# Scores of a chunked linear attention in four 64x64 tiles of TensorE, without the block above the diagonal

## The chip, the core and the metric

The kernel runs on one core of a Trainium2 chip. The metric is the device time of one execution in microseconds; of the runs of the kernel before, three are shown. An execution that the hardware profiler took is shown beside them: its time is compared with its own span, and all durations below come from it.

The engines are named as in the profile: PE (TensorE, matrix products), PEld (its weight loads), DVE (VectorE), ACT (ScalarE), POOL (GpSimd), SP (SyncE, which issues all loads and stores). Every engine works off its own list of instructions in order, and waits on semaphores for the others.

## The reference

A recurrence over 768 tokens for 4 batches and 8 heads of 48 channels, and behind it a two-layer network over all 3072 tokens (384 to 2048 to 384 channels):

```python
    for t in range(S):
        kt, vt, rt = (k[:, :, t], v[:, :, t], r[:, :, t])
        cur = np.einsum('bhd,bhe->bhde', u[None] * kt, vt)
        y[:, :, t] = np.einsum('bhd,bhde->bhe', rt, state + cur)
        state = w[None, :, :, None] * state + np.einsum('bhd,bhe->bhde', kt, vt)
...
    h = x @ w_in
    g = np.maximum(h, 0.0) + alpha * np.minimum(h, 0.0)
    return (g @ w_out).astype(np.float32)
```

## The kernel before, in words

**Attention.** The 768 tokens are cut into 6 chunks (`c`) of 128, and the heads into 4 pairs (`q`), which gives 24 stages; one call of `attention(c, q, at)` writes one stage. A stage loads `r` and `k0` (channels on the partitions: head 0 of the pair on partitions 0 to 47, head 1 on 64 to 111) and `v` and `k` (tokens on the partitions). DVE multiplies `r` and `k0` by tables of decay (L348). PE forms the scores `A[g]`, for each head `g` of the pair and each of the 4 batches a product of 128 by 128 tokens over 48 channels in f32 (L388, 8 products). Only scores of an earlier token with a later one are wanted, and the diagonal has a value of its own, `cu`. So ACT writes `base`, the identity scaled by `cu` (L395, 8 instructions), and DVE copies the scores above the diagonal into it under the mask `strict` (L399, `copy_predicated`, one instruction of 512 columns for each head). PE then multiplies state and `r` (L435), `v` and `base` (L440), and adds to the state (L449); in chunks 0 and 1 the first two are L429 and L424. ACT and DVE split the result into a high and a low part `xh`, `xl` (L482, L483).

In chunks 0 and 1 `cu` comes from a product on PE (L363: it needs `uw`, which POOL makes of the loaded `up` and `wp`, L242, and the product `prod` of DVE, L356); from chunk 2 on from POOL (L373, L375) and DVE (L379).

**Network.** 96 steps, each with 9 products of 512 columns into `hp` (L530) and 9 into `acc` (L561). ACT and DVE make the activations between them (L536, L537, L540, L541). The weights are split into high and low parts while the first steps run, one of 16 pieces at a time (L291 to L302; `wraw` is their load).

**Order.** Nothing runs in the order of the code. Each piece of work is given to a planner (`Plan`) with an engine, an assumed duration and a rank; it lists them by a simulation of its own and writes them out in that order. A piece whose assumed duration changes, a buffer pool of another size or an added piece can therefore move others on every queue. At the start, before there are products to do, PE is given small products of the identity (L621) to fill its waits. The pool `raw` (6 buffers) holds `r` and `k0`; those of stage 3 of chunk 0 lie in the pool `o`.

## Time and profile before

| | us |
|---|---|
| three runs, median (lowest to highest) | 525.99 (523.62 to 526.05) |
| the profiled execution, its time | 525.11 |
| the profiled execution, its span from first to last instruction | 523.4 |
| PE busy in it | 511.0 |
| DVE busy | 318.7 |
| ACT busy | 242.4 |
| POOL busy | 43.4 |

The time of an execution is its span and 1.7 us around it. A busy engine is read against a stretch, not the whole: an engine that is busy over half the span can be full in one stretch and idle in another. PE's rows overlap, since a product's end is modelled and the next begins before it; what one group of products costs is read from its first start to the first start of the next group.

### The profile page before, as it was taken

To read this page: it belongs to the slowest core of one execution; us is meant where nothing else is said; L and a number is where in the kernel's file an instruction comes from. 1 tells how busy PE (TensorE), PEld (TensorE's weight loads), DVE (VectorE), ACT (ScalarE), POOL (GpSimd) and SP (SyncE) were. 2 spreads that over 40 slices of the span, in tenths; PEclk is the share of its full clock that TensorE was granted. 3 is DMA by queue.
4 is the path that set the end of the run, shared out by engine and by line. 5 is a ranking of instruction groups with operands and counts; after the bars stand their busy time and mean duration, and the time that the engine had idled before them with its cause. 6 is when DMAs were issued, how large, how long until landed. Compare 5 with 4: busy or idle time off the path is not lost.

```text
span 523.4 us, 8460 instructions
## 1 busy us (share of the span) xinstructions
PE 511.0 (98%) x3288; PEld 406.3 (78%) x3288; DVE 318.7 (61%) x513; ACT 242.4 (46%) x525; POOL 43.4 (8%) x45
## 2 busy tenths in 40 slices
PE   7999999999999999999999999999999999999995
PEld 5877787888878777887787877877777778888883
DVE  5698999999556685854764654573544443333331
ACT  2766666658445352542552643552534332432222
POOL 1000030001012021120110102030000000000000
PEclk9699999999999999999999999999999999999998
DMA  8766666362232541422220323120120000100001
GB/s 224 271 180 195 209 195 206 107 224 91 74 107 81 168 144 35 145 69 66 75 61 20 111 71 88 48 82 1 35 92 2 0 1 2 60 0 1 0 1 64
DMA packets 24877, 47.22 MB, mean 90 GB/s; under 512 B 4096, under 2 KB 12416, under 8 KB 24832
## 3 DMA queue, kind: packets, MB, share of 16 engines
q1 hardware_dynamic: 24832, 46.62, 28.2%
q8 instruction: 28, 0.46, 0.4%
q14 instruction: 17, 0.14, 0.1%
HBM read 37.96 MB, written 6.29 MB: 85 GB/s over the span
## 4 chain that ended last, share of the span: by engine, by line
PE 93%; DMA 2%; DVE 2%; SPq 1%; issue 1%; ACT 0%; POOL 0%; ACTq 0%; POOLq 0%
PE acc L561 38%; PE hp L530 38%; PE A L388 5%; PE y L440 2%; PE y L435 2%; PE A L440 1%; PE acc L621 1%; PE y L424 1%; DMA wraw<-wall 1%; PE y L449 1%; DMA up<-uP 1%; PE acc L363 1%; PE y L429 1%; PE acc L388 1%; PE y L363 1%; DVE wx L298 1%
## 5 line engine op out<-in xcount | busy, mean ns | idle before, releaser
L537 DVE SCALAR_TENSOR_TENSOR g<-hp,alph,g 128x512 f32<-128x512 f32 x96 | 71.9, 749 | 127.0 <-ACT g L536 127.0
L536 ACT ACTIVATE g<-hp 128x512 f32<-128x512 f32 x96 | 57.3, 597 | 155.0 <-PE hp L530 154.7
L530 PE MATMUL hp<-xh,wh 128*128 128x512 f32 x288 | 116.3, 404 | 0.0
L530 PE MATMUL hp<-xl,wh 128*128 128x512 f32 x288 | 113.9, 395 | 0.3 <-DVE xl L483 0.3
L530 PE MATMUL hp<-xh,wl 128*128 128x512 f32 x288 | 114.0, 396 | 0.0
L540 ACT ACTIVATE gh<-g 128x512 fp32r<-128x512 f32 x96 | 60.5, 631 | 68.2 <-DVE g L537 68.1
L541 DVE TENSOR_TENSOR gl<-g,gh 128x512 fp32r<-128x512 f32 x96 | 66.6, 693 | 39.4 <-ACT gh L540 39.4
L561 PE MATMUL acc<-gh,wh 128*128 128x512 f32 x288 | 85.2, 403 | 0.6 <-ACT gh L540 0.6
L561 PE MATMUL acc<-gl,wh 128*128 128x512 f32 x288 | 83.2, 396 | 0.0
L561 PE MATMUL acc<-gh,wl 128*128 128x512 f32 x288 | 83.1, 395 | 0.0
L530 PEld LDWEIGHTS hp<-xh,wh 128*128 128x128 f32 x288 | 54.1, 188 | 13.9 <-issue 0.4
L530 PEld LDWEIGHTS hp<-xl,wh 128*128 128x128 f32 x288 | 54.2, 188 | 13.6 <-DVE xl L483 0.8
L561 PEld LDWEIGHTS acc<-gl,wh 128*128 128x128 f32 x288 | 54.1, 188 | 13.1
L561 PEld LDWEIGHTS acc<-gh,wl 128*128 128x128 f32 x288 | 54.1, 188 | 12.9
L561 PEld LDWEIGHTS acc<-gh,wh 128*128 128x128 f32 x288 | 52.5, 188 | 14.4 <-ACT gh L540 1.3
L530 PEld LDWEIGHTS hp<-xh,wl 128*128 128x128 f32 x288 | 54.2, 188 | 12.1
L395 ACT ACTIVATE base<-ident,cu 128x128 f32<-128x128 f32 x192 | 60.0, 390 | 0.2
L373 POOL TENSOR_TENSOR rr<-rr,kk 128x384 f32<-128x384 f32 x16 | 22.5, 1408 | 298.6 <-DMA kk<-vkr 180.1
L348 DVE TENSOR_TENSOR raw<-raw,W 112x512 f32<-112x512 f32 x46 | 35.5, 787 | 0.8 <-DMA raw<-rk 0.8
L399 DVE COPY_PREDICATED base<-strict,A 128x512 f32<-128x512 uint8 x44 | 30.3, 730 | 3.6 <-ACT base L395 1.8
L388 PEld LDWEIGHTS A<-raw 48*128 48x128 f32 x352 | 22.1, 193 | 8.3 <-issue 6.2
L388 PE MATMUL A<-raw 48*128 48x128 f32 x352 | 26.3, 290 | 1.3 <-DVE raw L348 1.3
(90 smaller groups left out, 420.8 us busy)
## 6 DMA issues: line engine op xcount, KB each, us to landing
wraw<-wall SPq DMA_DIRECT2D x16, 768.0 KB, 5.2
raw<-rk SPq DMA_DIRECT2D x46, 224.0 KB, 3.2
v<-vkr SPq DMA_DIRECT2D x24, 192.0 KB, 3.2
kk<-vkr SPq DMA_DIRECT2D x24, 192.0 KB, 2.7
rr<-vkr SPq DMA_DIRECT2D x16, 192.0 KB, 2.4
oT<-o SPq DMA_DIRECT2D x12, 256.0 KB, 2.2
oT<-g SPq DMA_DIRECT2D x6, 256.0 KB, 2.3
xh<-xh SPq DMA_DIRECT2D x36, 32.0 KB, 2.0
```

The source lines that it names most:

```text
L348: add("DVE", 0.72, lambda t=t, tab=tab: nc.vector.tensor_tensor(out=t(), in0=t(), in1=tab().broadcast_to([112, B, L]), op=ALU.mult), r=[W[ ...
L373: add("POOL", 1.2, lambda: nc.gpsimd.tensor_tensor(out=rt(), in0=rt(), in1=k(), op=ALU.mult), r=[k] + ([wh[12]] if c == 2 else []), w=[rt] ...
L388: nc.tensor.matmul(A[g]()[:, b], k0()[half(g), b], r()[half(g), b], start=(b == 0), stop=(b == B - 1), skip_group_check=True)
L395: add("ACT", 0.39, lambda g=g, b=b: nc.scalar.activation(base[g]()[:, b], ident(), AF.Copy, scale=cu()[:, g, b:b + 1]), r=[cu, ident], w=[ ...
L399: add("DVE", 0.75, lambda g=g: nc.vector.copy_predicated(base[g](), strict()[:, None, :].broadcast_to([128, B, L]), A[g]()), r=[strict, A[ ...
L440: nc.tensor.matmul(y[g]()[half(o), j * L:(j + 1) * L], v()[:, g * B + b], base[g]()[:, b], start=False, stop=(j == 1), skip_group_check=True)
L530: nc.tensor.matmul(hp(), a[i]()[:, k], x[c]()[:, k], start=(k == 0 and j == 0), stop=(k == NK - 1 and j == 2))
L536: add("ACT", 0.6, lambda: nc.scalar.activation(g(), hp(), AF.Copy), r=[hp], w=[g], rank=n - 100)
L537: add("DVE", 0.75, lambda: nc.vector.scalar_tensor_tensor(out=g(), in0=hp(), scalar=alph()[:, i:i + 1], in1=g(), op0=ALU.mult, op1=ALU.max ...
L540: add("ACT", 0.64, lambda: nc.scalar.activation(gh(), g(), AF.Copy), r=[g], w=[gh], rank=n - 100)
L541: add("DVE", 0.73, lambda: nc.vector.tensor_tensor(out=gl(), in0=g(), in1=gh(), op=ALU.subtract), r=[g, gh], w=[gl], rank=n - 99)
L561: nc.tensor.matmul(banks[k](), a[i]()[:, NK + k], x(), start=(begin and j == 0), stop=(end and j == 2))
```

## The change

Chunks 0 and 1 keep their products, masks and layout but for the order of the batches in `v`, `k` and `r`. From chunk 2 on (16 stages):

- The scores are formed by `triangle()`. Each product of 128 by 128 tokens becomes two: earlier tokens 0 to 63 with all 128 later ones, and earlier tokens 64 to 127 with later ones 64 to 127. The fourth block, earlier tokens 64 to 127 with later ones 0 to 63, is left out. Each product uses 48 channels and 64 columns of weights, so that it takes one of four quarters of PE; four stand in a row that use four different quarters (two heads, two batches).
- So that two batches can write the two halves of the partitions of one bank at a time, batches 1 and 3 have the two halves of a chunk's tokens swapped on the partitions. The host lays `v`, `k` and `r` of these batches out that way (`np.roll` by 64) and orders the batches 0, 2, 1, 3; `place` finds them. ACT writes `base` with its halves swapped, POOL makes a mask `strict4` with the swap in it and a second, swapped copy of the table `wtok` (`swapped_masks`), and `scale_k` reads the table with both.
- DVE's two copies under the mask become six: for each head the later tokens 64 to 127 on all partitions (256 columns), and for the even and for the odd batches the later tokens 0 to 63 on half the partitions (128 columns).
- The pool `raw` has 5 buffers; `k0` of stage 2 of chunk 0 lies in the pool `gl`.
- The planner is told 0.85 us for the scores in place of 1.1, and 0.42, 0.28 and 0.28 us for the copies of a head in place of 0.75.

```diff
+    strict4 = fixed([128, B, L], "strict4", U8)
...
-    wtok, w128, unit = fixed([128, H, D], "wtok"), fixed([112, P], "w128"), fixed([112, 65], "unit")
+    wtok, w128, unit = fixed([128, H, 2, D], "wtok"), fixed([112, P], "w128"), fixed([112, 65], "unit")
...
+    def swapped_masks():
+        add("POOL", 0.3, lambda: nc.gpsimd.memset(ones(), 1.0), w=[ones], rank=10)
+        for rows, base in ((slice(0, HI), -HI), (slice(HI, 128), 0)):
+            add("POOL", 0.3, lambda rows=rows, base=base: nc.gpsimd.affine_select(
+                ones()[rows], ones()[rows], pattern=[[1, 128]], base=base, channel_multiplier=-1,
+                compare_op=ALU.is_gt, fill=0.0), w=[ones], rank=10)
+        for b in range(B):
+            add("POOL", 0.3, lambda b=b: nc.gpsimd.tensor_copy(strict4()[:, b], (ones if b % 2 else strict)()),
+                r=[ones, strict], w=[(strict4, b)], rank=10)
+        for h in range(2):
+            add("POOL", 0.5, lambda h=h: nc.gpsimd.tensor_copy(
+                wtok()[HI * h:HI * h + HI, :, 1], wtok()[HI - HI * h:128 - HI * h, :, 0]), r=[(wtok, 0)],
+                w=[(wtok, 1 + h)], rank=10)
...
-        r, k0 = (sb([112, B, L], *(("o", 2) if first and q == P - 1 else ("raw", 6)))
-                 for _ in range(2))
+        place = [0, 2, 1, 3]
+        def swap(b):
+            return c > 1 and b % 2 == 1
+        r, k0 = (sb([112, B, L], *(("o", 2) if first and q == P - 1 else ("gl", 3) if first and q == 2 and j else
+                                   ("raw", 5))) for j in range(2))
...
+        def triangle():
+            for rows, j in ((0, 0), (0, 1), (1, 0), (1, 1)):
+                for b, g in ((2 * j, 0), (2 * j + 1, 0), (2 * j, 1), (2 * j + 1, 1)):
+                    o, t = (rows + b) % 2, slice(HI * rows, L)
+                    nc.tensor.matmul(A[g]()[HI * o:HI * o + HI, b, t], k0()[half(g), b, HI * rows:HI * rows + HI],
+                                     r()[half(g), b, t], start=(rows == 0 and j == 0), stop=(rows == 1 and j == 1),
+                                     skip_group_check=True)
         def scores():
+            if c > 1:
+                return triangle()
...
-        add("PE", 1.1, scores, r=[r, k0], w=A, rank=10 * q - 90 if first else at)
+        add("PE", 1.1 if c < 2 else 0.85, scores, r=[r, k0], w=A, rank=10 * q - 90 if first else at)
...
-                    base[g]()[:, b], ident(), AF.Copy, scale=cu()[:, g, b:b + 1]), r=[cu, ident], w=[(base[g], b)],
+                    base[g]()[:, b].rearrange("p (a t) -> p a t", a=2),
+                    ident().rearrange("p (a t) -> p a t", a=2)[:, ::-1 if swap(b) else 1], AF.Copy,
+                    scale=cu()[:, g, (b if c < 2 else place[b]):][:, 0:1]), r=[cu, ident], w=[(base[g], b)],
...
+        parts = [(slice(0, 128), slice(0, B), slice(HI, L)), (slice(0, HI), slice(0, B, 2), slice(0, HI)),
+                 (slice(HI, 128), slice(1, B, 2), slice(0, HI))]
+        for g, at_part in [(g, x) for g in range(2) for x in parts] if c > 1 else ():
+            add("DVE", 0.42 if at_part is parts[0] else 0.28, lambda g=g, x=at_part: nc.vector.copy_predicated(
+                base[g]()[x], strict4()[x], A[g]()[x]), r=[strict4, A[g]], w=[base[g]], rank=at - 1.5)
+        for g in range(2) if c < 2 else ():
...
-                    nc.tensor.matmul(y[g]()[half(o), j * L:(j + 1) * L], v()[:, g * B + b], base[g]()[:, b],
+                    nc.tensor.matmul(y[g]()[half(o), j * L:(j + 1) * L], v()[:, g * B + place[b]], base[g]()[:, b],
...
-            k4 = k().rearrange("p (g b) e -> p g b e", g=2)
+            table = wtok()[:, 2 * q:2 * q + 2, 0] if c < 2 else \
+                wtok()[:, 2 * q:2 * q + 2].rearrange("p h s e -> p (h s) e")
+            k4 = k().rearrange("p (n b) e -> p n b e", n=2 if c < 2 else 4)
...
+    swapped_masks()
...
-    vkr = np.ascontiguousarray(vkr.transpose(4, 2, 5, 0, 3, 1, 6)).reshape(C, H // 2, L, 3 * 2 * B * D)
+    vkr = vkr.transpose(4, 2, 5, 0, 3, 1, 6)[:, :, :, :, :, [0, 2, 1, 3]]
+    vkr = np.ascontiguousarray(vkr)
+    vkr[2:, :, :, :, :, 2:] = np.roll(vkr[2:, :, :, :, :, 2:], HI, axis=2)
+    vkr = vkr.reshape(C, H // 2, L, 3 * 2 * B * D)
```

What the planner makes of it is shown at three places. First PE's list, at the scores of chunk 2, pair 1; `hp` and `acc` belong to the network, `A0` and `A1` are the scores of the two heads. Before, the two rows of L388 stand four times in turn:

```order
L530 MATMUL hp_1712<-xl_426,wh14_98 128x512
L388 MATMUL A0_1727<-raw_961,raw_976 128x128
L388 MATMUL A1_1729<-raw_961,raw_976 128x128
L561 MATMUL acc0_1582<-gh_1627,wh12_96 128x512
L561 MATMUL acc1_1584<-gh_1627,wh12_96 128x512
```

And now, where each of the four rows of L411 stands twice, the two of 64x128 ahead of the two of 64x64, and `x2` is two batches:

```order
L571 MATMUL hp_1731<-xl_432,wh14_99 128x512
L411 MATMUL A0_1746<-raw_970,raw_1093 64x128 x2
L411 MATMUL A1_1749<-raw_970,raw_1093 64x128 x2
L411 MATMUL A0_1746<-raw_970,raw_1093 64x64 x2
L411 MATMUL A1_1749<-raw_970,raw_1093 64x64 x2
L602 MATMUL acc0_1601<-gh_1646,wh12_97 128x512
```

8 products have become 16 in the same place between the same products of the network. Second DVE's list, at a stage of chunk 3 (`T0` is the state, `xl0` the low part of the result; L537 and L541 belong to the network). Before:

```order
L537 SCALAR_TENSOR_TENSOR g_2193<-hp_2172,alph_71,g_2193 128x512
L541 TENSOR_TENSOR gl_2214<-g_2193,gh_2202 128x512
L399 COPY_PREDICATED base_1977<-strict_69,A0_2204 128x512
L399 COPY_PREDICATED base_2006<-strict_69,A1_2206 128x512
L537 SCALAR_TENSOR_TENSOR g_2231<-hp_2216,alph_71,g_2231 128x512
L541 TENSOR_TENSOR gl_2268<-g_2231,gh_2240 128x512
```

And now, where each row of 64x2x64 stands twice, for the even and the odd batches:

```order
L578 SCALAR_TENSOR_TENSOR g_2248<-hp_2229,alph_72,g_2248 128x512
L582 TENSOR_TENSOR gl_2277<-g_2248,gh_2257 128x512
L435 COPY_PREDICATED base_2020<-strict4_70,A0_2259 128x4x64
L435 COPY_PREDICATED base_2049<-strict4_70,A1_2262 128x4x64
L435 COPY_PREDICATED base_2020<-strict4_70,A0_2259 64x2x64
L435 COPY_PREDICATED base_2049<-strict4_70,A1_2262 64x2x64
L578 SCALAR_TENSOR_TENSOR g_2298<-hp_2279,alph_72,g_2298 128x512
```

Two copies have become six in the same place, and the network's next instruction stands behind them as before. Third SP's list of loads at the program's start, behind the first three loads of `raw`. Before:

```order
L221 DMA wp_64<-wP 112x4
L328 DMA raw_171<-rk 112x512
L328 DMA raw_173<-rk 112x512
L328 DMA o_175<-rk 112x512
L222 DMA up_65<-uP 112x4
L328 DMA raw_178<-rk 112x512
```

And now:

```order
L223 DMA wp_64<-wP 112x4
L349 DMA raw_170<-rk 112x512
L224 DMA up_65<-uP 112x4
L349 DMA o_177<-rk 112x512
L349 DMA raw_180<-rk 112x512
L349 DMA gl_186<-rk 112x512
```

The small load of `up` has moved two places ahead: one load of 112x512 stands between it and `wp`, where three stood. POOL's seven instructions for `strict4` stand ahead of `uw` on its list, and the two for `wtok` behind it. Between 20 and 100 us the planner has also exchanged neighbours on PE, DVE and SP in chunk 1; the visits of PE to products of another tile shape than the network's have become one more there.

## Rows read from the trace of the kernel before

**Rows 1.** The page: busy time of the engines; the chain that ended last, by engine.

```profile
PE 511.0 (98%) x3288; PEld 406.3 (78%) x3288; DVE 318.7 (61%) x513; ACT 242.4 (46%) x525; POOL 43.4 (8%) x45
...
PE 93%; DMA 2%; DVE 2%; SPq 1%; issue 1%; ACT 0%; POOL 0%; ACTq 0%; POOLq 0%
```

**Rows 2.** Stretches: length, busy us (instructions) of each engine, granted clock, DMA share, GB/s.

```profile
12.00:22.00 10.00, 9.73 (x67) 8.45 (x67) 5.89 (x15) 6.40 (x23) 0.00 (x0) 0.50 0.97 319
22.00:34.00 12.00, 11.73 (x138) 9.77 (x136) 11.29 (x18) 9.54 (x26) 0.00 (x0) 1.00 0.46 141
34.00:57.50 23.50, 21.76 (x202) 16.36 (x198) 22.11 (x35) 14.28 (x31) 0.00 (x0) 1.00 0.64 192
57.50:91.00 33.50, 33.50 (x288) 26.77 (x288) 33.25 (x49) 21.89 (x46) 5.94 (x4) 1.00 0.64 211
91.00:130.00 39.00, 39.00 (x175) 31.45 (x172) 37.74 (x60) 27.08 (x51) 2.24 (x2) 1.00 0.45 147
200.00:300.00 100.00, 100.00 (x675) 79.24 (x674) 59.72 (x100) 44.26 (x102) 11.80 (x10) 1.00 0.24 74
```

**Rows 3.** PE in order of time (start, us) around one stage's scores.

```profile
257.57 0.39 PE L530 MATMUL hp<-xh,wl 128*128 128x512 f32 x1
257.80 0.40 PE L530 MATMUL hp<-xl,wh 128*128 128x512 f32 x1
258.13 1.16 PE L388 MATMUL A<-raw 48*128 48x128 f32 x16
259.22 0.97 PE L561 MATMUL acc<-gh,wh 128*128 128x512 f32 x3
```

**Rows 4.** The scores' products by line: duration ns min/median/max, first and last start.

```profile
L388 PE MATMUL A<-raw x352: 271/272/579, 8.5 to 420.2; 48*128 48x128 f32 x176
```

**Rows 5.** PE in order of time at the same stage's products behind the scores.

```profile
263.61 0.31 PE L435 MATMUL y<-raw,T 48*48 48x128 f32 x1
263.63 0.31 PE L435 MATMUL A<-raw,T 48*48 48x128 f32 x1
263.76 0.27 PE L435 MATMUL y<-raw,T 48*48 48x128 f32 x1
263.87 0.27 PE L435 MATMUL y<-raw,T 48*48 48x128 f32 x1
263.98 0.27 PE L435 MATMUL y<-raw,T 48*48 48x128 f32 x1
264.20 0.31 PE L440 MATMUL y<-base,v 128*48 128x128 f32 x1
...
265.11 0.61 PE L449 MATMUL y<-v,kk 128*64 128x48 f32 x16
265.65 0.96 PE L561 MATMUL acc<-gh,wh 128*128 128x512 f32 x3
```

**Rows 6.** Groups by line: count, busy us, mean ns of one, idle before.

```profile
L399 DVE COPY_PREDICATED base<-strict,A 128x512 f32<-128x512 uint8 x44 | 30.3, 730 | 3.6 <-ACT base L395 1.8 <-PE A L388 1.8
L483 DVE TENSOR_TENSOR xl<-A,xh 48x256 fp32r<-48x256 f32 x32 | 13.5, 423 | 4.5 <-ACT xh L482 3.3
L375 POOL TENSOR_TENSOR rr<-rr,utab 128x384 f32<-128x384 f32 x16 | 18.7, 1169 | 1.3
```

**Rows 7.** DVE in order of time behind the scores of rows 3.

```profile
259.60 1.35 DVE L399 COPY_PREDICATED base<-strict,A 128x512 f32<-128x512 uint8 x2
260.84 0.67 DVE L541 TENSOR_TENSOR gl<-g,gh 128x512 fp32r<-128x512 f32 x1
264.41 0.75 DVE L537 SCALAR_TENSOR_TENSOR g<-hp,alph,g 128x512 f32<-128x512 f32 x1 [2.90 <-ACT g L536]
```

**Rows 8.** The chain that ended last, at the start: start, us, what.

```profile
4.09 5.51 DMA up<-uP
...
10.59 1.05 PE acc L363 x8
```

**Rows 9.** DVE and POOL at the start, in order of time, with waits.

```profile
5.74 0.48 DVE L247 TENSOR_TENSOR_SCAN W<-wp,unit 112x65 f32<-112x65 f32 x2 [4.59 <-DMA wp<-wP]
...
8.92 0.69 DVE L356 TENSOR_TENSOR g<-raw 112x512 f32<-112x512 f32 x1
...
1.82 0.29 POOL L237 CAST strict<-ones 128x128 uint8<-128x128 f32 x1
...
9.75 0.79 POOL L242 TENSOR_TENSOR uw<-up,wp 48x4 f32<-48x4 f32 x2 [7.56 <-DMA up<-uP]
```

More of the change, by code (lines that the diff above doesn't have):

```diff
@@ L265, in token_table @@
         add("DVE", 0.4, lambda: nc.vector.tensor_copy(
-            wtok().rearrange("p (m g) e -> p m g e", g=2), pt()[:, :, :, 0:D]), r=[pt], w=[wtok], rank=-30)
+            wtok()[:, :, 0].rearrange("p (m g) e -> p m g e", g=2), pt()[:, :, :, 0:D]), r=[pt], w=[(wtok, 0)], rank=-30)
     raws = {}
@@ L395, in attention @@
                 add("ACT", 0.39, lambda g=g, b=b: nc.scalar.activation(
-                    base[g]()[:, b], ident(), AF.Copy, scale=cu()[:, g, b:b + 1]), r=[cu, ident], w=[(base[g], b)],
+                    base[g]()[:, b].rearrange("p (a t) -> p a t", a=2),
+                    ident().rearrange("p (a t) -> p a t", a=2)[:, ::-1 if swap(b) else 1], AF.Copy,
+                    scale=cu()[:, g, (b if c < 2 else place[b]):][:, 0:1]), r=[cu, ident], w=[(base[g], b)],
                     rank=at - 0.9 if c != 1 else -50)
-        for g in range(2):
+        parts = [(slice(0, 128), slice(0, B), slice(HI, L)), (slice(0, HI), slice(0, B, 2), slice(0, HI)),
[4 more added lines that the diff above has]
+        for g in range(2) if c < 2 else ():
             add("DVE", 0.75, lambda g=g: nc.vector.copy_predicated(
@@ L422, in out @@
                     for g in range(2):
-                        rows, x = (slice(0, HI) if g == 0 else half(g)), g * B + b
+                        rows, x = (slice(0, HI) if g == 0 else half(g)), g * B + place[b]
                         nc.tensor.matmul(y()[rows, b], v().rearrange("p x e -> p (x e)")[
@@ L447, in state_product @@
                 for g in range(2):
-                    rows, x = slice(HI * g, HI if g == 0 else HI + D), g * B + b
+                    rows, x = slice(HI * g, HI if g == 0 else HI + D), g * B + place[b]
                     nc.tensor.matmul(u_rows(rows)[:, b], kt[:, x * D:x * D + rows.stop - rows.start], vt[:, x],
@@ L456, in scale_k @@
         def scale_k():
-            k4 = k().rearrange("p (g b) e -> p g b e", g=2)
+            table = wtok()[:, 2 * q:2 * q + 2, 0] if c < 2 else \
+                wtok()[:, 2 * q:2 * q + 2].rearrange("p h s e -> p (h s) e")
+            k4 = k().rearrange("p (n b) e -> p n b e", n=2 if c < 2 else 4)
             nc.vector.tensor_tensor(out=k4, in0=k4, op=ALU.mult,
-                                    in1=wtok()[:, 2 * q:2 * q + 2, None, :].broadcast_to([128, 2, B, D]))
+                                    in1=table[:, :, None, :].broadcast_to(list(k4.shape)))
         if first:
@@ L464, in attention @@
             if not last:
-                add("DVE", 0.56, scale_k, r=[wtok], w=[k], rank=at - 1.6)
+                add("DVE", 0.56, scale_k, r=[(wtok, 0)] if c < 2 else [wtok], w=[k], rank=at - 1.6)
             add("PE", 1.7 if last else 2.3, out if last else both, r=[T[q], r, v] + base + ([] if last else [k]),
@@ L510, in state @@
                 U = pb([112, B * D], "y")
-                add("DVE", 0.56, scale_k, r=[wtok], w=[k], rank=0.5 * q - 1)
+                add("DVE", 0.56, scale_k, r=[(wtok, 0)], w=[k], rank=0.5 * q - 1)
                 add("PE", 0.8, state_product, r=[k, v], w=[U], rank=0.5 * q - 1)
```

## The prediction

> **What bounds the kernel now.** I read the page's busy times first, then the stretches, then PE's own timeline. The page gives PE 511.0 us of a span of 523.4, and the chain of work that ended last runs through PE for 93% of the span; no other engine is over 61% [rows 1]. A mean over stages says little, so the second view is the stretches [rows 2]: from 57.5 us on PE's busy time equals the length of every stretch shown (33.50 of 33.50, 39.00 of 39.00, 100.00 of 100.00), at a granted clock of 1.00, which is 2.4 GHz. There PE waits for nobody, and a microsecond less of work on PE is a microsecond less of time. Before 57.5 it is otherwise: between 34 and 57.5 PE is busy for 21.76 of 23.50 us and DVE for 22.11, between 22 and 34 DVE for 11.29 of 12, and from 57.5 to 91 DVE is as full as PE (33.25 of 33.50). All 16 stages that the change touches lie behind chunk 1, in the part that PE bounds; the change reaches the first 57 us only through the planner.
>
> **The scores on PE.** One stage before: its 16 records (8 products, two records each) begin at 258.13 and the network's next product at 259.22, so the scores hold PE for 1.09 us [rows 3]. The scores' rows on `A` number 352 [rows 4], with 32 more on other banks for the 24 stages, so 16 a stage everywhere.
>
> One stage after has 32 records. The nearest row for the first 16 (64 columns of weights, 128 columns passed through, 48 rows, four quarters of PE) is L435, which works in the same four quarters on the same `raw` with 48 columns of weights: it begins at 263.61, the next line at 264.20, so 0.59 us for 16 records, with entry and exit [rows 5]. The four quarters start within 0.02 us of each other (263.61 to 263.63), and the steps of one quarter follow at 0.11 us (263.76, 263.87, 263.98). The 16 columns more of weights count once, ahead of the first step; a third of what the first step is longer by (263.76 - 263.61 - 0.11 = 0.04) makes 0.01.
>
> The other 16 records pass 64 columns instead of 128, in four further steps. Upper bound of a step: 0.11, as if the shorter pass gained nothing. Lower bound: half, 0.055. Which one holds depends on whether 64 columns of weights can be loaded into each quarter at that pace. L449 shows it for two halves of PE: 16 records, 8 in each half, one half with 64 columns of weights and 48 passed; the first starts at 265.11, the last at 265.11 + 0.61 - 0.22 = 265.50 (0.22 for the length of one record), which is 7 steps of 0.056 [rows 5]. I take 0.056, since it is the row with the same weights.
>
> So a stage after is 0.59 + 0.01 + 4 x 0.056 = 0.82, between 0.82 and 0.59 + 0.01 + 4 x 0.11 = 1.04. Gain: 1.09 - 0.82 = 0.27 at best, 0.05 at worst. Entry and exit are the same before and after: a product of the network stands on either side, as before. I round down to 0.26, as four quarters with short passes are shown by no row: **16 x 0.26 = 4.2 us**, with 0.8 as the other end.
>
> A rule of the Trainium skill speaks against this: "TensorE: Matmul & The Clock Gate", section "Wait — 56ns, not 53.3ns?", says that products never start less than about 25 ns apart however short they are. By it the 16 short records would take 0.40 us, the stage 1.00, and the gain would be an estimated 16 x 0.09 = 1.4 us. The trace disagrees for quarters that are free: four starts within 0.02 us [rows 5].
>
> **DVE.** Two copies of 512 columns at 0.73 us become six [rows 6]. No row shows the smaller ones. A copy of 256 columns out of a PSUM bank takes 0.42 in L483 [rows 6]; by the slope between the two (0.31 for 256 columns) one of 128 columns takes 0.27, and at most 0.42. A stage then costs 2 x (0.42 + 2 x 0.27) = 1.92 to 2 x 3 x 0.42 = 2.52 in place of 1.46: 0.5 to 1.1 us more, 7 to 17 us in all. None of it is on the path. Behind the copies DVE sits idle for 2.90 us ahead of 264.41, and the copies end at 260.95 where L440, which reads them, begins at 264.20 [rows 5, 7]: 3.25 us of cover for 1.1. Queued behind the copies is L541 (260.84), whose result is used steps later. Without the cover the price would be the whole 17 us. In the fullest stretch (91 to 130, DVE 37.74 of 39.00 [rows 2]) lies one stage's set, whose 0.5 to 1.1 still fits in 1.26.
>
> **ACT** writes the same 8 blocks with halves swapped. Even at twice the price it would stay off the path: ACT is busy for 44 of 100 us [rows 2]. `scale_k` multiplies the same number of elements. Counted at nothing.
>
> **POOL and the loads at the start.** Seven instructions for `strict4` stand ahead of `uw` on POOL: by L237's 0.29 us [rows 9] 2.0 us at most. POOL waits there for 7.56 us for `up` [rows 9], which hides them; without that wait they would delay `uw` by 2.0. And `up` itself is now two loads earlier. `wp` landed at about 5.7 us, when DVE's L247 could start [rows 9], `up` at 9.60 [rows 8], with three loads of 224 KB between: 1.3 us each. With one between, `up` lands near 7.0 and `uw` is ready near 7.9. The first L363 then waits for `prod` (L356, 8.92 + 0.69 = 9.61 [rows 9]) and starts near 9.7 instead of 10.59 [rows 8]. This is the head of the chain that ended last, so I take **0.9 us** off; between nothing (if a later wait, for ACT or a load, takes its place) and more (see the clock, below).
>
> **What the planner moved between 20 and 100 us.** One more visit of PE to another tile shape costs about 0.2 us: 0.33 between 257.80 and 258.13 where the network's step is 0.23, and the same again behind it [rows 3]. POOL's two copies for `wtok` run right behind DVE's making of that table in chunk 0, at most 1.17 each (L375 [rows 6]), while DVE is nearly full; nobody waits for them until chunk 2, but the two can slow each other. And neighbours on DVE's list have been exchanged where it is full. I bound this sum by -0.5 and +1.5 and take **+0.5**.
>
> Sum, against the profiled execution: 525.1 - 4.2 - 0.9 + 0.5 = 520.5. The median of the runs is 0.9 above that execution, 525.99. Halfway between them is 525.5, from which the sum gives 520.9; I forecast **521.0**, and count the rivals from 525.5 too.
>
> **The rivals.**
> - *Short products gain nothing much.* The 0.024 us from record to record in L449 (0.39 us for 16) is also what one would see if PE could not start records faster in a sustained row. Then the 16 short records take 0.39 in place of 0.22, or, at the upper bound above, 0.44: a stage of 0.99 to 1.04, a gain of 0.8 to 1.6 us. For it: no row has 32 such records. Against it: in L449 the weights of 64 columns explain the same step. Time: 525.5 - 1.2 - 0.4 = 523.9. This is also how the change would fail to do what it says.
> - *The clock does not fall at the start.* From 12 to 22 us PE runs at 0.50, 1.2 GHz, and DVE is busy for only 5.89 of 10 us [rows 2]; ahead of it PE waited for `raw` and for `uw`. With `uw` early, PE's wait shrinks by 0.9, and the clock may stay up. PE's 10 us of work would take 5; DVE's 4.1 idle us cap the gain. Half of the cap, 2, on top of the forecast: 519.0.
> - *A wait opens in 34 to 57.5.* There DVE has 1.4 us to spare in 23.5 [rows 2], and its order has changed. If PE waits there for a split piece of weights for as long as it did ahead of 12 us (some 2 us in all), the clock can fall again for as long as it did then: ten microseconds at half, 5 us. With the start's gain lost as well, 525.5 - 4.2 + 0.5 + 5 = 526.8, slower than before. Against it: DVE's work ahead of the weights is the same but for about one instruction.
>
> **How the numbers follow.** The forecast has 0.58 (519.5 to 522.8), the short products 0.19, the clock 0.14, the wait 0.09. The range should leave out the wait and the tails: 518.3 to 524.3. About 0.5% (2.6 us) is what a measurement of this kernel can tell from no change. Forecast and clock lie below 523.4 with little exception, 0.70; the short products are within, with the forecast's tail and half of the third rival's, 0.24; slower is the rest, 0.06.
>
> **What would show it.** In the profile after: a stage's scores from first start to the network's next product at 0.80 to 0.85 (0.99 or more: the first rival); the quarters' short steps at 0.056; PE's busy time equal to the stretches from about 57 us on; L363's first start near 9.7; L435's copies done before L440. The prediction is wrong if PE shows waits behind 57.5 us, if the last product of chunk 1 ends later than before, or if the short steps are 0.1 us.

## The result: 517.3 us, below the range

The changed kernel takes 517.30 us (median of its runs, 516.91 to 518.28); the runs of the kernel before beside it have a median of 524.81 (520.12 to 526.05). The ratio is 0.9874, with a 95% interval of 0.9844 to 0.9905: 1.3% shorter, clear of noise, by more than the forecast of 521.0, and below the range of 518.3 to 524.3. Over the 70 runs of the kernel before that stand beside the experiments its median is 523.77, so the 525.5 from which the forecast counted was 1.7 too high: the first fault of the prediction, and one that no view of a single profile shows.

### The profile page after: what moved, and what is told of

The parts are those of the page before. It is cut to its first block, busy times and chain, and to the rows that moved or that the text cites. A ratio compares the mean times of both kernels' runs of the same rounds, so it can differ in the third digit from the quotient of the medians.

```text
span 515.2 us, 9052 instructions
## 1 busy us (share of the span) xinstructions
PE 504.3 (98%) x3544; PEld 400.8 (78%) x3544; DVE 328.2 (64%) x577; ACT 242.8 (47%) x525; POOL 46.9 (9%) x54
## 4 chain that ended last, share of the span: by engine, by line
PE 93%; DVE 3%; ACT 1%; DMA 1%; issue 1%; SPq 0%; DVEq 0%; ACTq 0%
PE acc L602 39%; PE hp L571 39%; PE A L411 3%; PE y L479 2%; PE y L474 2%; PE A L479 1%; PE A L420 1%; PE y L463 1%; PE y L488 1%; PE y L468 1%; ACT base L427 1%; DMA wp<-wP 1%; PE acc L384 1%; DVE raw L369 1%; PE acc L662 1%
## 5 line engine op out<-in xcount | busy, mean ns | idle before, releaser
L571 PE MATMUL hp<-xh,wh 128*128 128x512 f32 x288 | 115.7, 402 | 0.8 <-DMA xh<-xh 0.8
L571 PE MATMUL hp<-xl,wh 128*128 128x512 f32 x288 | 113.8, 395 | 0.0
L571 PE MATMUL hp<-xh,wl 128*128 128x512 f32 x288 | 113.7, 395 | 0.0
L582 DVE TENSOR_TENSOR gl<-g,gh 128x512 fp32r<-128x512 f32 x96 | 68.6, 714 | 41.5 <-ACT gh L581 41.3
L602 PE MATMUL acc<-gh,wh 128*128 128x512 f32 x288 | 85.2, 402 | 0.2 <-ACT gh L581 0.2
L602 PE MATMUL acc<-gh,wl 128*128 128x512 f32 x288 | 83.3, 396 | 0.0
L602 PE MATMUL acc<-gl,wh 128*128 128x512 f32 x288 | 82.7, 394 | 0.0
L571 PEld LDWEIGHTS hp<-xh,wh 128*128 128x128 f32 x288 | 54.0, 188 | 14.4 <-DMA xl<-xl 0.9
L602 PEld LDWEIGHTS acc<-gl,wh 128*128 128x128 f32 x288 | 54.0, 188 | 12.8
L602 PEld LDWEIGHTS acc<-gh,wl 128*128 128x128 f32 x288 | 53.8, 188 | 13.0
L571 PEld LDWEIGHTS hp<-xl,wh 128*128 128x128 f32 x288 | 54.1, 188 | 12.7
L571 PEld LDWEIGHTS hp<-xh,wl 128*128 128x128 f32 x288 | 54.1, 188 | 12.0
L602 PEld LDWEIGHTS acc<-gh,wh 128*128 128x128 f32 x288 | 52.4, 188 | 13.3 <-ACT gh L581 0.7
L394 POOL TENSOR_TENSOR rr<-rr,kk 128x384 f32<-128x384 f32 x16 | 20.4, 1273 | 275.0 <-DMA kk<-vkr 136.5
L369 DVE TENSOR_TENSOR raw<-raw,W 112x512 f32<-112x512 f32 x45 | 36.7, 832 | 0.0
L435 DVE COPY_PREDICATED base<-strict,A 64x128 f32<-64x128 uint8 (+1 forms) x96 | 26.9, 343 | 0.8
L524 DVE TENSOR_TENSOR xl<-y,xh 48x256 fp32r<-48x256 f32 (+1 forms) x38 | 17.5, 462 | 3.0 <-ACT xh L523 2.6
L396 POOL TENSOR_TENSOR rr<-rr,utab 128x384 f32<-128x384 f32 x16 | 19.2, 1202 | 1.3
```

The source lines that it names most:

```text
L369: add("DVE", 0.72, lambda t=t, tab=tab: nc.vector.tensor_tensor(out=t(), in0=t(), in1=tab().broadcast_to([112, B, L]), op=ALU.mult), r=[W[ ...
L394: add("POOL", 1.2, lambda: nc.gpsimd.tensor_tensor(out=rt(), in0=rt(), in1=k(), op=ALU.mult), r=[k] + ([wh[12]] if c == 2 else []), w=[rt] ...
L396: add("POOL", 1.2, lambda: nc.gpsimd.tensor_tensor(out=rt().rearrange("p (g b) e -> p g b e", g=2), in0=rt().rearrange("p (g b) e -> p g b ...
L435: add("DVE", 0.42 if at_part is parts[0] else 0.28, lambda g=g, x=at_part: nc.vector.copy_predicated(base[g]()[x], strict4()[x], A[g]()[x] ...
L524: add("DVE", us + 0.1, lambda: nc.vector.tensor_tensor(out=view(l), in0=psum(), in1=view(h), op=ALU.subtract), r=[src] + refs(h), w=refs(l ...
L571: nc.tensor.matmul(hp(), a[i]()[:, k], x[c]()[:, k], start=(k == 0 and j == 0), stop=(k == NK - 1 and j == 2))
```

## The profile after

The profiled execution took 516.91 us, 515.2 of them in the span. In the changed file the scores of chunk 2 and on are L411 (those of chunks 0 and 1 stay in L420), the network's products L571 and L602, the products with `uw` L384, the new predicated copies L435, the products behind the scores L474, L479 and L488. The page's busy times and its chain by engine (answering rows 1):

```profile
PE 504.3 (98%) x3544; PEld 400.8 (78%) x3544; DVE 328.2 (64%) x577; ACT 242.8 (47%) x525; POOL 46.9 (9%) x54
PE 93%; DVE 3%; ACT 1%; DMA 1%; issue 1%; SPq 0%; DVEq 0%; ACTq 0%
```

The bound is the same: PE, 6.7 us less busy than before. The stretches (answering rows 2; length, then busy us of PE, PE's weight loads, DVE, ACT, POOL, then the granted clock, DMA share and GB/s):

```profile
12.00:22.00 10.00, 9.56 (x79) 7.85 (x79) 7.85 (x19) 7.60 (x25) 0.00 (x0) 0.66 1.04 319
22.00:34.00 12.00, 11.34 (x131) 9.35 (x131) 11.41 (x18) 8.86 (x23) 3.27 (x2) 1.00 0.53 155
34.00:57.50 23.50, 22.80 (x188) 17.25 (x188) 23.27 (x37) 15.20 (x36) 0.00 (x0) 1.00 0.62 207
57.50:91.00 33.50, 33.50 (x310) 27.05 (x310) 33.00 (x51) 21.07 (x41) 5.66 (x4) 1.00 0.65 205
91.00:130.00 39.00, 39.00 (x170) 31.45 (x169) 38.32 (x61) 27.91 (x51) 2.23 (x2) 1.00 0.39 132
200.00:300.00 100.00, 100.00 (x762) 79.29 (x761) 62.80 (x125) 44.92 (x103) 11.30 (x10) 1.00 0.25 78
```

From 57.5 us on PE is busy for the whole of each stretch, as before. What differs is the start: the granted clock of 12 to 22 is 0.66 where it was 0.50, and PE works 22.80 us of 34 to 57.5 where it worked 21.76. PE around one stage's scores (answering rows 3), and the two shapes of L411 (count, busy us, mean ns):

```profile
252.38 0.40 PE L571 MATMUL hp<-xl,wh 128*128 128x512 f32 x1
252.71 0.90 PE L411 MATMUL A<-raw 48*64 48x128 f32 x32
253.54 0.97 PE L602 MATMUL acc<-gh,wh 128*128 128x512 f32 x3
...
L411 PE MATMUL A<-raw 48*64 48x128 f32 x256 | 10.7, 282 | 0.0
L411 PE MATMUL A<-raw 48*64 48x64 f32 x256 | 6.6, 218 | 0.0
```

From the first start to the network's next product: 253.54 - 252.71 = 0.83, against 1.09 before. The 0.33 ahead of it (252.38 to 252.71) is the same entry as before.

DVE behind these scores, and the first product behind them that has to do with the copies (answering rows 5 to 7):

```profile
254.18 1.67 DVE L435 COPY_PREDICATED base<-strict,A 128x256 f32<-128x256 uint8 x6
255.88 0.69 DVE L582 TENSOR_TENSOR gl<-g,gh 128x512 fp32r<-128x512 f32 x1
...
257.93 0.31 PE L474 MATMUL A<-raw,T 48*48 48x128 f32 x1
```

Six copies take 1.67 where two took 1.35, and end 2.08 us ahead of L474 (257.93 - 255.85), the first to write into the bank `A` that they read.

The two ends of the start: POOL's `uw`, PE's first products with it (answering rows 8 and 9), and the first scores of chunk 2, which come at 90.36 before:

```profile
7.13 0.94 POOL L258 TENSOR_TENSOR uw<-up,wp 48x4 f32<-48x4 f32 x2 [2.92 <-DMA up<-uP]
...
9.96 1.02 PE L384 MATMUL acc<-uw,g 112*128 112x2 f32 x8
...
87.13 0.90 PE L411 MATMUL A<-raw 48*64 48x128 f32 x32
```

```profile
90.36 1.16 PE L388 MATMUL A<-raw 48*128 48x128 f32 x16
```

So of the 8.2 us between the two spans, 3.23 have been gained by the first scores of chunk 2, and 4.97 behind them (523.4 - 90.36 = 433.04; 515.2 - 87.13 = 428.07). Behind PE's last product stand the last copy and store, 6.4 us in the one profile and 6.6 in the other, so PE's own part is counted up to that product. Before, then after:

```profile
516.56 0.40 PE L561 MATMUL acc<-gl,wh 128*128 128x512 f32 x1
```

```profile
508.20 0.39 PE L602 MATMUL acc<-gl,wh 128*128 128x512 f32 x1
```

From the first scores of chunk 2 to its end that is 516.96 - 90.36 = 426.60 before and 508.59 - 87.13 = 421.46 after: 5.1 us. The 16 stages give 16 x 0.26 = 4.2 of them. Two things are left to find: the rest of 0.9 behind chunk 1, and the 3.2 of the start.

PE's waits in the two profiles (what waited and for whom: us in sum, times, longest), of before the two that went, and then those of after, but for the 1.4 us at the very start that both have:

```profile
PE acc L363 <- POOL uw L242: 1.0, 1, 1.0
...
PE y L363 <- DVE xl L483: 0.6, 1, 0.6
```

```profile
PE A L420 <- DVE raw L369: 0.9, 1, 0.9
PE hp L571 <- DMA xh<-xh: 0.8, 1, 0.8
PE acc L662 <- ACT cu L388: 0.7, 2, 0.4
PE acc L602 <- ACT gh L581: 0.2, 1, 0.2
```

The wait for `uw` is gone and so is that of L363 for DVE's `xl` near 55 us; a wait for a load of `xh` (0.8 us, near 34) is new.

## The experiments

To keep start and rest apart, each profile is cut at the first scores of chunk 2. The table is worked out from their rows and the spans; "network" is the time of 17 steps of the network (18 products each) near the end, as read below. Behind PE's last product 6.2 to 6.9 us pass in these profiles, in no order that goes with the edits, so the column up to that product is the one to compare.

```
profile                        clock 12-22  first scores  from there  to PE's last  network
                                            of chunk 2    to the end  product
before                         0.50         90.36         433.0       426.6         71.40
e1  raw 5, one k0 in gl        0.50         88.67         432.6       425.8         71.17
e2  up early                   0.66         87.36         433.3       426.6         71.40
e10 before, 7 fillers more     0.66         87.68         432.9       426.7         71.40
after                          0.66         87.13         428.1       421.5         71.17
e3  after, up late             0.50         88.72         428.0       421.5         71.17
e9  after, 5 fillers more      0.83         86.42         427.8       421.5         71.17
e4  after, whole second half   0.66         87.41         431.1       424.8         71.17
e5  after, no swap             0.52         89.59         430.9       424.7         71.17
e11 after, copies twice        0.66         87.01         431.8       425.4         71.17
e12 after, that k0 in g        0.71         94.01         429.2       422.5         71.40
```

### The scores: whole second half, and no swap

The second-half products pass all 128 columns instead of 64 (the 64 extra are the block that the change leaves out, earlier tokens 64 to 127 with later ones 0 to 63; nobody reads them):

```
-                    o, t = (rows + b) % 2, slice(HI * rows, L)
+                    o, t = (rows + b) % 2, slice(0, L)
```

> The changed kernel, but the second half's products pass all 128 later tokens instead of 64, so that the block above the diagonal is computed after all (it is not copied on). Theory (a short step lasts as long as its weights, half a long one): a stage's scores take 0.83 + 4 x 0.055 = 1.05 us, time 16 x 0.22 = 3.5 us over the changed kernel, 520.8. Rival (the gain comes from the four quarters alone, short steps are bound by the rate at which records start): 0.83 to 0.90 and no more than 1 us over.

Without the swap every batch writes the same half of `A`'s partitions for the same tokens, and long and short products take turns; the loads, `wtok`, the masks and the copies follow:

```
-            for rows, j in ((0, 0), (0, 1), (1, 0), (1, 1)):
-                for b, g in ((2 * j, 0), (2 * j + 1, 0), (2 * j, 1), (2 * j + 1, 1)):
-                    o, t = (rows + b) % 2, slice(HI * rows, L)
+            for b in range(B):
+                for g, rows in ((0, 0), (0, 1), (1, 0), (1, 1)):
+                    o, t = rows, slice(HI * rows, L)
...
```

> The changed kernel without the swap of the odd batches' token halves, and so with the rows of a batch's k on the same halves of the partitions for all batches. The same 32 records with the same numbers of columns, but all 128-column products go to one half of PE's columns and all 64-column products to the other; their order alternates between the two halves. Theory (the gain comes from an equal load on the four quarters): a quarter with the 128-column products has 8 records at 0.11, 0.88 us, and with the 0.2 of entry and exit a stage takes 1.05 to 1.10 as before the change, 0.24 more than after: 16 x 0.24 = 3.8 us above the changed kernel, 521.2 at a clock of 0.990. Rival (the gain comes from the fewer columns in sum, and PE starts the 64-column products in what the others leave): the stage stays at 0.83 to 0.90, 517 to 518.5.

PE around one stage's scores, with the whole second half and then without the swap:

```profile
254.44 1.10 PE L411 MATMUL A<-raw 48*64 48x128 f32 x32
255.48 0.97 PE L602 MATMUL acc<-gh,wh 128*128 128x512 f32 x3
```

```profile
256.58 1.10 PE L411 MATMUL A<-raw 48*64 48x128 f32 x32
257.61 0.97 PE L602 MATMUL acc<-gh,wh 128*128 128x512 f32 x3
```

Both stages take 1.03 or 1.04 in place of 0.83. The whole second half runs at 520.88 (ratio to before 0.9950, 0.9922 to 0.9978), the kernel without swap at 520.35 (0.9928, 0.9896 to 0.9959): 3.6 and 3.1 us above the changed kernel, for 16 x 0.2 = 3.2 expected from the rows. So the gain of the scores needs both: fewer columns, and the swap that gives each quarter of PE as many of the short products as of the long ones. The four quarters alone bring 0.06 of the 0.26 (1.09 to 1.03). Without the swap one half of the columns has all the long products, and that half alone sets the stage: in the trace its quarters start their long records 0.11 apart up to 257.41, while the last short one starts at 257.20, though the last product on PE's list is a short one.

### The copies twice

```
-                base[g]()[x], strict4()[x], A[g]()[x]), r=[strict4, A[g]], ...
+                base[g]()[x], strict4()[x], A[g]()[x]) for _ in range(2)], r=[strict4, A[g]], ...
```

> The changed kernel with each of the six predicated copies of a stage done twice in a row (the second writes the same values again): 16 stages x 6 x 0.28 us, 27 us more on DVE and nothing else moved. Theory (the copies lie beside PE's work with over 3 us of cover from chunk 3 on, and DVE is near full only in chunk 1 and at chunk 2's first stage): 0 to 2 us, 517.3 to 519.3, with any wait of PE ahead of 130 us. Rival (DVE's queue sets the second half): about 1.7 a stage, 27 us, 544.

It took 521.55 (0.9952, 0.9923 to 0.9981), 4.2 above the changed kernel: neither theory. DVE and PE around one stage of this run, and PE's wait in sum:

```profile
183.59 3.95 DVE L435 COPY_PREDICATED base<-strict,A 128x256 f32<-128x256 uint8 x12
186.26 0.42 PE L474 MATMUL y<-raw,T 48*48 48x128 f32 x2
187.69 0.28 PE L474 MATMUL A<-raw,T 48*48 48x128 f32 x1 [1.00 <-DVE base L435]
...
PE A L474 <- DVE base L435: 1.0, 1, 1.0
```

L474 has two outputs, `y` and `A`, and the second is written into the bank that the copies still read. It is L474 that waits, not L479. In the changed kernel the copies end between 1.8 and 2.6 us ahead of L474, from the second stage on (the first has far more); the doubling takes 2.3, so 8 of these 15 stages wait, 3.8 us in sum (the starts from L474 to L479 add up to 13.18 in place of 9.34). So the copies cost nothing as they are, and the cover is 1.8 to 2.6 us a stage, not the 3.25 of the prediction.

### The load of `up`

One kernel is that before with `up` issued two places earlier and nothing else; the other the changed kernel with `up` two places later, where it was.

```
+    loads = [p for p in order if p.eng == "SP"]
+    up_load = [p for p in loads if p.kb == 1][1]
+    behind = loads[4]                          # the changed kernel with up late: loads[7]
+    order.remove(up_load)
+    order.insert(order.index(behind) + 1, up_load)
```

> The kernel before with one edit: the small load of up is issued two places earlier, as in the changed kernel; everything else in its written order. Theory (early up is the cause of the start's gain): first L363 near 10.0 instead of 10.59, first L424 near 16.6 instead of 18.58, time 1.8 to 2.0 us under before; the wait of 1 us at 55 us stays. Rival (the start gains by what else moved, the load of raw behind o): first L424 within 0.5 us of 18.58.

> The changed kernel with one edit: the small load of up is issued two places later, where the kernel before has it. Theory: the start's gain goes, the first L463 is near 18.6 instead of 16.60, time 1.8 to 2.0 us over the changed kernel, 519.2. Rival (the order behind it takes that up again, since DVE is full from 20 us on): first L463 later, first scores of chunk 2 within 0.5 us of 87.13, time unchanged.

`up` early in the kernel before: 522.97 (0.9993, 0.9973 to 1.0014), 0.8 below the median of 523.8. `up` late in the changed kernel: 518.82 (0.9911, 0.9880 to 0.9943), 1.5 above the changed kernel's median. Both were expected at 1.8 to 2.0, and neither is clear of noise: the first interval holds 1, the second overlaps with that of the changed kernel (0.9844 to 0.9905). The first L363 moved from 10.59 to 9.66, where the prediction had 9.7. In these four profiles the granted clock of 12 to 22 went along: 0.66 with `up` early, 0.50 with it late (first fence: before with `up` early; second: after with `up` late):

```profile
12.00:22.00 10.00, 9.56 (x80) 7.87 (x82) 7.83 (x18) 7.55 (x24) 0.00 (x0) 0.66 1.01 324
```

```profile
12.00:22.00 10.00, 9.73 (x64) 8.07 (x60) 7.00 (x17) 6.84 (x23) 0.00 (x0) 0.50 0.95 311
```

That `up` sets the clock is not shown: runs of one kernel differ in it, and the table has the contrary too (e1 and e5 have `up` early and show 0.50 and 0.52, e10 has it late and shows 0.66). Carried to one mean granted clock (0.990, along the slope within the kernels, about 0.45 us for 0.001), `up` is worth 0.4 in the kernel before and 0.3 in the changed one. So some 0.3 to 0.4 can be put down to the shorter wait; what lies above that, to 0.8 and 1.5, went with the clock and is no better known than the medians.

### More filler at the start

Five more of the products on `ident` ahead of the first scores in the changed kernel, seven more in the kernel before:

```
-    add("PE", 7.0, lambda: [warm() for _ in range(33)], ...
+    add("PE", 7.0, lambda: [warm() for _ in range(38)], ...      # 40 in the kernel before
```

> The changed kernel with five more of PE's filler products (128x256 in bf16 on ident, results unused) in the row that PE runs at the start: 38 in place of 33, at 0.18 us each, into the 0.94 us in which PE waits ahead of the first scores (7.72 to 8.66). All else stands in the same order on every engine. Theory (that wait is what the fall of the granted clock to 0.50 at 12.98 follows): the stretch at half level goes or becomes shorter, and the time falls by half of its 6.8 us less what other engines set there: 1 to 3.4 us, 514 to 516.3. Rival (the fall has another cause, or the other engines set the time there anyway): 517.3 as before, the first L463 at 16.6.

> The kernel before with seven more filler products at the start (40 in place of 33), into the 1.27 us in which PE waits ahead of its first scores (7.18 to 8.45); nothing else moves. The wait for up at 9.62 to 10.59 stays. Theory (the wait ahead of the first scores alone leads to the fall of the clock): the stretch at half level of 10.2 us shrinks and the time falls by 2 to 4 us, 519.5 to 521.5. Rival (the wait for up is enough for it): the time stays at 523.5, the half level at 10 us.

PE's first scores with the wait ahead of them (e9, then e10; the clock of their starts is in the table):

```profile
8.82 1.16 PE L420 MATMUL A<-raw 48*128 48x128 f32 x16 [0.97 <-DVE raw L369]
```

```profile
8.84 1.16 PE L388 MATMUL A<-raw 48*128 48x128 f32 x16 [0.26 <-DVE raw L348]
```

In the changed kernel the median stayed: 517.45 (0.9876, 0.9812 to 0.9941), with runs from 515.98 to 518.28; the profiled one shows a short stretch at half level, but the wait was still there: 40 fillers took 6.40 us in that execution where 35 had taken 6.28, so nothing can be put down to them. In the kernel before the wait did shrink, from 1.27 to 0.26, and the median was 524.89 (1.0030, 0.9996 to 1.0064): no gain. The theory that the wait ahead of the first scores alone brings the clock down falls for the kernel before. In the changed kernel the edit did not remove the wait, but the profile with the copies twice (e11), whose start has the changed kernel's order, happens to have none: its 35 fillers took 6.84 us and ran up to the first scores.

```profile
1.44 6.84 PE L662 MATMUL acc<-ident 128*128 128x256 bf16 x35 [1.44 <-POOL uw L256]
8.35 1.16 PE L420 MATMUL A<-raw 48*128 48x128 f32 x16
```

The clock of 12 to 22 is 0.66 there all the same, as in the changed kernel with its wait of 0.94. So this wait alone is not the cause in that profile either; what brings the clock down was not found.

### The buffers: five of `raw`, one `k0` in `gl`

In the kernel before, the edit of the pools alone (e1), each of its halves (e6, e7), and a variant that gives `gl` three such `k0`, so that its three buffers come back into their former turn (e8):

```
-        r, k0 = (sb([112, B, L], *(("o", 2) if first and q == P - 1 else ("raw", 6)))
+        r, k0 = (sb([112, B, L], *(("o", 2) if first and q == P - 1 else
+                                   ("gl", 3) if first and q == 2 and j else ("raw", 5)))   # e1
+        ... else ("raw", 5)))                                                             # e6
+        ... else ("gl", 3) if first and q == 2 and j else ("raw", 6)))                    # e7
+        ... else ("gl", 3) if first and q < 3 and j else ("raw", 6)))                     # e8
```

> The kernel before with one edit: the pool raw has 5 buffers and k0 of stage 2 of chunk 0 lies in the pool gl. Scores, masks and copies are those of before; the planner's order in chunks 0 and 1 becomes almost that of the changed kernel (up two loads earlier, neighbours exchanged in chunk 1). Theory (the gain beyond the scores is the planner's order): the first L424 near 16.6 us instead of 18.58, the first scores of chunk 2 near 87.2 instead of 90.36, behind that the steps of before; time 3 us under the kernel before. Rival (the start's gain is chance, from how long the clock stays at half level): the first scores of chunk 2 within 1 us of 90.36 in the same state of the clock, time within 1 us of before. Rival (the scores bring more than their rows show): no gain here.

> The kernel before with 5 buffers of raw in place of 6, and nothing else: every tile behind raw lies 2 KB lower, gl stays the last tile, and the order in which the three buffers of gl are used is as before. What is read is the time of one step of the network (18 products of 128x512) in the steady part: 4.200 us in the kernel before and with the early load of up alone, 4.185 to 4.189 in the changed kernel and with the pool edit alone. If fewer buffers of raw (the addresses behind it, or the later loads) make the step shorter: 4.186. If it is the place of gl or its turn: 4.200. The time is within 522 to 525 either way.

> The kernel before with raw left at 6 buffers, and k0 of one stage of chunk 0 in a buffer of gl: gl then lies early, ahead of v, and its three buffers are used one turn later than before. If the place of gl or its turn makes the step shorter: 4.186 us. If it is the number of raw's buffers: 4.200.

> As the run with one k0 in gl, but with k0 of three stages of chunk 0 there: gl lies as early, and its three buffers come back to the turn that they have in the kernel before. If the place of gl makes the step shorter: 4.186 us. If its turn against the buffers of g and gh does: 4.200.

And in the changed kernel, that one `k0` in a buffer of `g`, all else as it is:

```
-   ("gl", 3) if first and q == 2 and j else ("raw", 5)
+   ("g", 3) if first and q == 2 and j else ("raw", 5)
```

> The changed kernel with the k0 of that one stage of chunk 0 in a buffer of g in place of gl. The gl buffers then lie at the end of the memory again, behind gh, as in the kernel before, and are used in the turn of the kernel before; raw keeps its 5 buffers and the scores their 64x64 tiles. Some neighbours in chunks 0 and 1 change places. Theory (the shorter step of the network, 4.186 in place of 4.200 us for 18 products, comes from where and when gl is used): 4.200 again, which over the 1,593 products behind chunk 1 is 1.0 to 1.2 us more time than the changed kernel's, 518.2 at a clock of 0.990, give or take what the start does. Rival (it comes from something else in the change): the step stays at 4.186 and the time near 517.1.

Two things came out of these. The first is the network's step. PE's rows of the product `acc<-gh,wh` 17 steps apart: before; after; e7; e8; e12.

```profile
430.70 0.86 PE L561 MATMUL acc<-gh,wh 128*128 128x512 f32 x3
...
502.10 0.86 PE L561 MATMUL acc<-gh,wh 128*128 128x512 f32 x3
```

```profile
430.99 0.86 PE L602 MATMUL acc<-gh,wh 128*128 128x512 f32 x3
...
502.16 0.86 PE L602 MATMUL acc<-gh,wh 128*128 128x512 f32 x3
```

```profile
432.68 0.86 PE L561 MATMUL acc<-gh,wh 128*128 128x512 f32 x3
...
503.85 0.86 PE L561 MATMUL acc<-gh,wh 128*128 128x512 f32 x3
```

```profile
429.59 0.86 PE L561 MATMUL acc<-gh,wh 128*128 128x512 f32 x3
...
500.88 0.86 PE L561 MATMUL acc<-gh,wh 128*128 128x512 f32 x3
```

```profile
430.21 0.86 PE L602 MATMUL acc<-gh,wh 128*128 128x512 f32 x3
...
501.61 0.86 PE L602 MATMUL acc<-gh,wh 128*128 128x512 f32 x3
```

17 steps take 71.40 before, 71.17 after and in e7, 71.29 in e8, and 71.40 again in e12 (and in e6): 4.200 or 4.186 us a step, with the same products in the same order and PE without a wait in all of them. What decides is whether that one `k0` lies in `gl`: e7 against before and e12 against the changed kernel differ in that edit alone and in the planner's order that follows from it. `raw`'s five buffers alone change nothing. By which way it acts is open. A pool's tiles lie in memory in the order in which the program first uses them: with a `k0` of chunk 0 in it, `gl` moves from the end, behind `gh`, to a place ahead of `v`, and the tiles between move up. In e8 the buffers of `gl` have their former turn, which gives half, but the tiles between also move otherwise than in e7; place, turn and these tiles were not told apart. Up to PE's last product it makes 0.8 us in the kernel before (426.6 against 425.8 in e1) and 1.0 in the changed one (422.5 in e12 against 421.5). Over the 88 steps the 0.23 of 17 steps would make 1.2; part of the steps between the stages gains less than those near the end.

The second is the start, and it is larger. e12 has all of the shorter scores and yet ran at 524.83 (1.0017, 0.9985 to 1.0049): the whole gain is gone. A load into `g` has to wait for a buffer that `g`'s other users release; in the planner's order it stands behind the first load of `wraw`, eight places later than the load into `gl` stood, and its neighbours on SP's list have moved with it: `up` is two places later. Two of its stretches, PE's largest waits, and its first scores of chunk 2:

```profile
22.00:34.00 12.00, 10.26 (x91) 8.67 (x88) 7.81 (x12) 8.78 (x26) 0.11 (x1) 0.72 0.67 213
57.50:91.00 33.50, 31.58 (x274) 25.13 (x272) 29.43 (x45) 18.90 (x44) 6.34 (x4) 1.00 0.51 160
...
PE acc L662 <- ACT cu L388: 2.2, 2, 1.7
PE acc L384 <- POOL uw L258: 1.9, 1, 1.9
PE acc L602 <- ACT gh L581: 1.9, 1, 1.9
...
94.01 0.90 PE L411 MATMUL A<-raw 48*64 48x128 f32 x32
```

PE waits for `uw` again, twice as long as before, the clock falls a second time between 22 and 34, and a wait of 1.9 opens even behind 57.5: the scores of chunk 2 begin 6.9 us later than in the changed kernel. e7 (526.93, one run) shows another way in which it can go, with the clock at full over 12 to 22 us and down later:

```profile
34.00:57.50 23.50, 19.29 (x122) 15.23 (x122) 19.33 (x29) 12.57 (x29) 0.00 (x0) 0.78 0.65 217
```

e6 took 527.68 and e8 523.86, one run each. e1 ran at 522.91 (0.9973, 0.9957 to 0.9990), 0.9 below the kernel before in place of the 3 that its theory expected; some 0.4 of its time lies outside its span (2.12 us between time and span, 1.75 elsewhere). At one mean granted clock (0.990) it is 1.5 below. So the edit of the pools, with the early `up` that comes of it, brings a part of what the scores leave over, 0.8 of it by the shorter step.

## Where the prediction was right and where not

**The bound, and the scores.** Right: a stage forecast at 0.82 takes 0.83, and 16 x 0.26 = 4.2 us. The short steps of the quarters go at the pace taken from L449, and the first rival (0.99 to 1.04 a stage) is out. What it would have looked like is e4: 1.03. The rule weighed there, from the Trainium skill's "TensorE: Matmul & The Clock Gate", section "Wait — 56ns, not 53.3ns?", would have given an estimated 1.00; the trace does not agree for quarters of PE: the stage takes 0.83, and its 32 records start within 0.90 - 0.22 = 0.68 us, 0.022 apart on the mean, the long ones included.

**DVE, ACT, POOL.** Nothing on the path, as said. The page's busy time of DVE grew by 9.5 us (forecast 7 to 17). The cover was read to the wrong reader: L440, which reads `base`, where L435, which overwrites `A`, comes first. The rows of `A<-raw,T` stood in rows 5. It made no difference at the real cost, and 4 us with the copies doubled.

**The start.** `uw` was ready near 8.1 (forecast 7.9), the first L384 came at 9.96 (forecast 9.7), and the medians moved by 0.8 and 1.5 with `up` alone (forecast 0.9), neither clear of noise. The second rival, that the clock does not fall, is not borne out: in the one pair of profiles the clock over 12 to 22 us is 0.66 in place of 0.50, but the mean granted clock of the 70 runs before and of the four after is the same, 0.989.

**The base.** The forecast counted from 525.5, between the profiled execution and the median of three runs. Both were long draws: the 70 runs of the kernel before lie between 520.4 at a mean granted clock of 0.995 and 528.6 at 0.980, 15 of them are as long as the profiled execution or longer, and six as long as the 525.99 of the three other runs. In every profile here PE runs at 1.2 GHz only in the first 60 us and behind its last product, so the mean clock says mostly how long that stretch at the start was; 0.50 over the whole of 12 to 22 in the profile before was a long one. The range should have held a microsecond or two for that alone.

**The planner's moves: the step that failed, beside the base.** It was put at +0.5, between -0.5 and +1.5, from three small costs, and the edit of the buffers was not priced as a part of its own. In its place the runs show -0.8 to -1.0: the network's shorter step, in a part that the prediction took as unchanged because its instructions are. The cause is shown as far as the edit goes (e1 and e7 have it, e6 and e12 have not); why the step is shorter stays open. The sum then closes: 523.8 less 4.2 (scores), 0.9 (step) and 0.8 to 1.5 (`up`) is 517.2 to 517.9, against 517.3. Of the miss of 3.7 us, 1.7 are the base and 1.4 this term; had either been right, the time would have lain within the range. The remaining 0.6 lies within what the runs with `up` leave open. That nothing else is left for the planner's moves is a sum, not a run of its own.

**The third rival**, a wait in 34 to 57.5 that brings the clock down, did not happen here. That such a start can happen shows in e7, with a clock of 0.78 over 34 to 57.5 and PE busy for 19.29 of 23.50 us there: 3.2 us above the kernel before, in one run. In e12 the second fall lies earlier, between 22 and 34, and the kernel is 7.5 above the changed one. The 5 that was put on the rival lies between. In both it hung on which buffer one `k0` was given.

No kernel run here is faster than the changed one; that with five fillers more (517.45) cannot be told from it.

## What to carry to other kernels

Price an edit of pools and buffers as a change in itself: read which load has to wait for which buffer and what is then behind it on the queue, and expect the whole start to move with it; here the choice of one tile's pool was worth 7 us, more than the change in the arithmetic. Where a buffer is overwritten, count the cover to the writer that comes first, not to the reader of the result. And before summing against one profiled execution, look whether it is a typical run: a stretch at half clock whose length varies makes three runs a poor base for a sum of one-microsecond terms.

## What was not expected of the hardware

Products on quarters of PE run side by side: in this kernel 32 records on 64x64 tiles (16 products of two records each), half of them of 128 and half of 64 columns, take 0.83 us with entry and exit, where 16 records of full width took 1.09, and a quarter that gets only the long ones holds the other up (1.03). The interval between two products of 128x512 that run without any wait is not a constant of their shape: 17 steps of 18 products took 71.40 us in five kernels and 71.17 in eight others with the same products in the same order (71.29 in one), going with whether one early tile shares the pool of one operand (`gl`); why was not found. The same program, run again, has another mean granted clock (0.980 to 0.995 over 70 runs of the kernel before), and 0.001 of it went with about 0.45 us.
